# Pooled attention and a rational MoE layer: rest products in row halves, fill into open sums, moved due times

## The chip, the cores and the metric

The kernel runs on one core of a Trainium2 chip. The metric is the device time of one execution, in microseconds.

## The reference

Attention with pooled keys and values feeds one feed-forward layer with a rational function in the middle.

```python
B, H, S, D = 8, 8, 576, 64
k_p = k.reshape(B, H, 72, 8, D).mean(axis=3)           # eight neighbours become one key
v_p = v.reshape(B, H, 72, 8, D).mean(axis=3)
scores = (q @ k_p^T) / sqrt(D)
attn = exp(scores - max);  attn /= sum(attn) + 1e-9
x = (attn @ v_p) as [B*S = 4608 tokens, H*D = 512]
h = x @ w_in                                            # 512 -> 2048
P = a[0] + a[1]*h + a[2]*h^2 + a[3]*h^3
Q = 1 + |b[0]|*|h| + |b[1]|*h^2
out = (P / (Q + 1e-6)) @ w_out                          # 2048 -> 512
```

All arrays are float32 except the two weight matrices, which come as 64-bit floats.

## The kernel before

**Blocks and units.** The 4608 tokens are 18 blocks of 256. The 2048 hidden columns are 8 units of 256. The list `order` says which blocks meet which unit when: blocks 0 to 3 one by one at first, while the weights arrive, and from block 4 on (with block 1 again) in overlapping pairs, so that every block is in two neighbouring pairs, with four of the units in each. `mm1` multiplies a block (or a pair, 512 columns at once) with `w_in`, `rational` computes P/Q on ScalarE, VectorE and GpSimd, and `mm2` adds the products with `w_out` to the block's two open sums `po`, which `deliver` writes out at the end.

**Precision.** Products run in fp32r, a float32 format that TensorE takes in one pass. Where that is not precise enough a value is split into a high and a low part, and three products (high x high, low x high, high x low) are added. So `x`, the weights, `gh`/`gl`, the attention weights `am` and the pooled values `vm` all stand twice.

**Attention of a block.** `prep_k` and `prep_v` load and pool keys and values of a batch (`prep_v_early`, for the first two batches, lets TensorE do the pooling). `attention` computes scores `ps`, the softmax in tile `e`, and the transposed weights in `am` (by TensorE transposes for blocks 0 to 3, by VectorE's 32x32 transposes and DMAs after that). `values` multiplies them with the pooled values into the banks `pv`, and two copies by ScalarE and VectorE split the result into `x`.

**The rest of the keys.** Two heads share one product: 2 x 72 = 144 keys. 128 of them fill the array's rows, and the last REM = 16 are left over. For these rests there is a product of its own, whose 128 rows hold four copies (index g) of two pairs of heads (index m) of 16 rows (index r). The four copies hold the four combinations of high and low parts of weights and values, so that one product adds them all at once. Before, the rows are ordered (g, m, r). The product of one pair of heads uses all 128 rows with the other pair's masked to zero: `vr` has one masked version for each of the four pairs, made with the columns `mrem_lo` and `mrem` of `masks`. In `values`, for each half `c` of the heads, pair `jj` and batch segment, four products go to one `pv` bank: two with `vm`, one with `vr`, one with `vm`. A block that crosses a batch boundary has two segments, so its products are shorter and twice as many.

**What sets the order.** Nothing is issued in program order. `Plan.add` records each operation with its engine, an estimated cost, and a due time `plan.now`. `Plan.solve` first hands due times back to the operations that others depend on, then goes through time with those costs and picks for each engine the operation that can start first, with a small weight on due times. It also hands out the buffers: PSUM has 8 banks (pool `ps`), and an operation can start only when it gets all banks that it touches first. `Plan.issue` writes out the order, one in-order queue per engine; semaphores keep dependencies. Loads are all on SyncE's queue.

**Fill.** Where the plan has TensorE wait, `issue` puts in dummy products of 256 columns with the identity `identr` (`self.filler`), priced at 0.12 us. Up to the last operation on the bank `idle` (due at 96 us) they go into that bank, which nothing else can use until then; after that, up to FILL = 110 us of plan time, into a fresh bank just before the operation that will overwrite it.

Helper `Plan.issue` issues nearly everything, so most instructions carry line L267, and fill carries L264. They are told apart by tile.

Of the kernel before, what the change touches and what calls it, by code (L numbers as in the profile page):

```python
# [8 lines left out]
F32 = mybir.dt.float32  # L9
# [85 lines left out]
class Op:  # L95
    __slots__ = ("eng", "cost", "port", "calls", "deps", "users", "bufs", "due", "wait",
                 "ready", "seq", "bytes", "early", "slack", "start", "end")


class Plan:  # L100
# [5 lines left out]
    FILL = 110.0  # L106

    BETA = 0.02
# [13 lines left out]
    def add(self, eng, cost, calls, port=False, claims=(), bytes=0, early=34.0, after=()):  # L122
        op = Op()
        op.eng, op.cost, op.port, op.calls, op.bytes = eng, cost, port, calls, bytes
        op.early, op.slack = early, self.slack
# [24 lines left out]
        for b in op.bufs:  # L150
            b.left += 1
        self.ops.append(op)
        return op

    def solve(self):
        for op in reversed(self.ops):
            for d in op.deps:
                d.users.append(op)
                d.due = min(d.due, op.due - d.slack * (d.cost + 0.25 + (4.0 if d.bytes else 0.0)))
        for op in self.ops:  # L160
            op.wait, op.ready = len(op.deps), max(0.0, op.due - op.early)
# [9 lines left out]
        while done < len(self.ops):  # L171
# [58 lines left out]
            for u in op.users:  # L230
                u.wait -= 1
                u.ready = max(u.ready, op.end + (self.LAT if u.eng != op.eng else 0.0))
                if not u.wait:
                    engs[u.eng].append(u)
# [4 lines left out]
    def issue(self):  # L239
        for op in self.order:  # L240
            for b in op.bufs:
                b.it = None
        engines = {"sp": self.nc.sync, "act": self.nc.scalar, "actq": self.nc.scalar,
                   "dve": self.nc.vector, "pool": self.nc.gpsimd, "pe": self.nc.tensor}
        value = lambda v: v.ap() if isinstance(v, Lazy) else v
        free, steady = None, [o.start for o in self.order if self.idle.tile in o.bufs][-1]
        for op in self.order:
            if op.eng == "pe" and op.start <= self.FILL:


                to = self.idle.ap() if op.start <= steady else None
                dst = op.calls[0][1][0]
                if to is None and dst.tile.it is None and dst.tile.dtype == F32:
                    to = dst.ap()
                one = self.filler
                if to is not None and tuple(to.shape) != (128, 128):
                    one = one.unsqueeze(1).to_broadcast([128, 2, 128])
                    if tuple(to.shape) not in ((128, 256), (128, 2, 128)):
                        to = None
                while free is not None and to is not None:  # L260
                    free += 0.12 if free > self.WARM else 0.215
                    if free > op.start - (0.0 if op.start <= steady else 0.2):
                        break
                    self.nc.tensor.matmul(to, lhsT=self.filler, rhs=one, start=True, stop=True)  # L264
                free = op.end
            for name, args, kw in op.calls:
                getattr(engines[op.eng], name)(*map(value, args),  # L267
                                               **{k: value(v) for k, v in kw.items()})
# [17 lines left out]
def tile_pooled_attention_then_rational_moe(  # L286
# [21 lines left out]
    G = 8  # L308
# [57 lines left out]
    masks = new("cpool", "masks", [P, 6], F32, "masks")  # L366
# [6 lines left out]
    mrem_lo, mrem = ([masks[:, i + m:i + m + 1] for m in range(2)] for i in (2, 4))  # L373
# [6 lines left out]
    def make_masks():  # L380
# [12 lines left out]

        for m in range(2):
            for g in range(4):
                band(bands[:, g:g + 1], g * 32 + m * REM, g * 32 + (m + 1) * REM)
            small("tensor_tensor", out=mrem_lo[m], in0=bands[:, 1:2], in1=bands[:, 3:4],
                  op=ALU.add)
            small("tensor_tensor", out=mrem[m], in0=bands[:, 0:1], in1=bands[:, 2:3], op=ALU.add)
            small("tensor_tensor", out=mrem[m], in0=mrem[m], in1=mrem_lo[m], op=ALU.add)  # L400
# [65 lines left out]
    vr = [new("cpool", f"vr{i}", [P, NJ, D], F32R, f"vr{i}") for i in range(2)]  # L466

    def prep_k(n):
# [5 lines left out]
        for c0, c1, np in ((0, 2, P), (2, 4, P), (4, 5, H * SP - 4 * P)):  # L474
# [9 lines left out]
            while w > D:  # L484
# [34 lines left out]
    def prep_v_early(n):  # L519
# [11 lines left out]
        for m in range(2):  # L531
            dma(64, place[m * REM:(m + 1) * REM, CW:2 * CW].rearrange("p (c x) -> p c x", c=2),
                rows[m::2, 0:REM, :].rearrange("c r x -> r c x"))
# [5 lines left out]
    def prep_v(n):  # L539
# [4 lines left out]
        for c in (2, 0, 1):  # L544
# [4 lines left out]
            else:  # L549
                for g in range(4):  # L550
                    for m in range(2):
                        p0 = g * 32 + m * REM
                        dma(64, place[p0:p0 + REM].rearrange("p (j x) -> p j x", j=2),
                            rows[m::2, 0:REM, :].rearrange("c r x -> r c x"))
# [10 lines left out]
    def split_v(n, vs, vrs, port):  # L565
# [44 lines left out]
    def attention(t, hi, lo, qs, es):  # L610

# [50 lines left out]
        rem = [pairs[:, 2 * c:2 * c + 2, 0:REM].unsqueeze(1).to_broadcast([P, 4, 2, REM])  # L662
               for c in range(2)]
        four = [pairs[:, NJ + c, REM:].rearrange("p (g m r) -> p g m r", g=4, m=2)
# [6 lines left out]
        else:  # L671
# [6 lines left out]
            for c in range(2):  # L678
# [4 lines left out]
            act(2 * P).copy(lo[:, NJ:, col], pr)  # L683
            dve(2 * P).tensor_tensor(
                out=lo[P // 2:, NJ:, col], in0=pr[P // 2:],
                in1=lo[P // 2:, NJ:, col].bitcast(F32), op=ALU.subtract)
# [36 lines left out]
    def attend(i):  # L723
# [12 lines left out]
        if i >= 4:  # L736
# [171 lines left out]
    for g in range(4):  # L908
        small("tensor_copy", out=fourfold[:, g * 32:(g + 1) * 32], in_=ident[:2 * REM, :2 * REM])
# [29 lines left out]
    plan.filler = identr  # L939
# [38 lines left out]
```

## Time and profile before

| | |
|---|---|
| median of 3 runs | 952.7 us (952.23 to 953.07) |
| profiled execution | 953.93 us, its span 952.2 us |
| TensorE products busy | 938.5 us, 99% of the span |
| VectorE, ScalarE, GpSimd busy | 83%, 73%, 55% |
| products | 4888 records, 160 of them on tile `idle` |
| mean granted TensorE clock | 0.997 |

The span runs from the first to the last instruction of the profiled execution. In the views below PE is TensorE's products and PEld its weight loads, which overlap the products; DVE is VectorE, ACT ScalarE, POOL GpSimd and SP SyncE. Records of products overlap too: a product's record ends when its last result has left the array, well after the next has begun. What a product costs on a full TensorE is therefore the distance from its start to the next start, not its mean duration.

### The profile page before, as it was taken

Reading aid. Unit: us, or ns where it says so; the run is one execution under the profiler, and the core shown is the slowest. Engines: PE = TensorE matmul, PEld = TensorE weight load, DVE = VectorE, ACT = ScalarE, POOL = GpSimd, SP = SyncE. Lnnn points to the kernel's source line nnn. Section 1 sums busy time; section 2 is a strip of 40 time slices with the busy share of each in tenths; the row PEclk is TensorE's granted clock in tenths of the full one; section 3 lists DMA queues with packets and bytes.
Section 4 is the critical chain, followed back from the end, with each engine's and each line's share of the span. In section 5 each row is a group of like instructions: output and inputs, shape, how many; then the busy total and the mean of one; then the engine's idle time right before and its main releaser. Section 6 shows DMA issues by size and latency. Waiting matters only on the chain.

```text
span 952.2 us, 14488 instructions
## 1 busy us (share of the span) xinstructions
PE 938.5 (99%) x4888; PEld 786.1 (83%) x4888; DVE 791.5 (83%) x1334; ACT 691.6 (73%) x1124; POOL 523.3 (55%) x463
## 2 busy tenths in 40 slices
PE   8999999999999999999999999999999999999997
PEld 7989999898878888877887888878887888888886
DVE  6978888988898888888888989888979878886664
ACT  4778788687767686767777686858586868586764
POOL 4676667874456453547454844465456544444442
PEclk9999999999999999999999999999999999999999
DMA  9993110551436130316031512162223312020001
GB/s 280 345 384 120 24 50 1 120 149 49 89 64 148 19 60 12 66 51 141 5 68 50 122 33 43 41 135 55 32 53 74 71 26 53 0 56 1 23 1 45
DMA packets 185354, 75.16 MB, mean 79 GB/s; under 512 B 162624, under 2 KB 162624, under 8 KB 185280
## 3 DMA queue, kind: packets, MB, share of 16 engines
q1 hardware_dynamic: 185280, 74.23, 31.6%
q8 instruction: 39, 0.64, 0.3%
q14 instruction: 35, 0.29, 0.1%
HBM read 50.60 MB, written 12.58 MB: 66 GB/s over the span
## 4 chain that ended last, share of the span: by engine, by line
PE 84%; DVE 6%; ACT 3%; SPq 2%; DMA 2%; issue 2%; POOL 1%; ACTq 0%; POOLq 0%; DVEq 0%
PE po L267 37%; PE ph L267 36%; PE pv L267 4%; PE ps L267 3%; SPq L267 2%; DVE t L267 2%; PE idle L264 1%; DVE m_win L267 1%; DVE sm L267 1%; DMA q<-in_q_dram 1%; PE pvs L267 1%; DMA st_v<-in_v_dram 1%; DVE e L267 1%; ACT t L267 1%; ACT rp L267 1%
## 5 line engine op out<-in xcount | busy, mean ns | idle before, releaser
L267 PE MATMUL ph<-x,win 128*128 128x512 f32 (+1 forms) x2112 | 469.9, 354 | 4.8 <-DVE t L267 1.8
L267 PEld LDWEIGHTS ph<-x,win 128*128 128x128 f32 x2112 | 355.1, 188 | 72.6 <-DVE t L267 3.6
L267 PE MATMUL po<-wout,gh 128*128 128x512 f32 x1152 | 329.6, 397 | 0.3 <-ACT gh L267 0.3
L267 POOL TENSOR_TENSOR w<-w,r 128x512 f32<-128x512 f32 (+1 forms) x145 | 190.8, 1316 | 243.4 <-ACT r L267 228.9
L267 PEld LDWEIGHTS po<-wout,gh 128*128 128x128 f32 x1152 | 208.5, 188 | 42.1 <-ACT gh L267 0.5
L267 POOL TENSOR_TENSOR gl<-t,gh 128x512 fp32r<-128x512 f32 (+1 forms) x145 | 189.0, 1304 | 97.3 <-ACT gh L267 93.5
L267 PE MATMUL po<-wout,gl 128*128 128x512 f32 x576 | 167.6, 397 | 0.0
L267 ACT ACTIVATE t<-ph,abn 128x512 f32<-128x512 f32 (+1 forms) x145 | 111.7, 771 | 41.0 <-PE ph L267 30.8
L267 ACT ACTIVATE rp<-w,cbias 128x512 f32<-128x512 f32 (+1 forms) x145 | 99.7, 688 | 57.4 <-POOL w L267 24.3
L267 DVE TENSOR_TENSOR t<-t,ph 128x512 f32<-128x512 f32 (+1 forms) x145 | 98.4, 678 | 50.0 <-ACT t L267 48.0
L267 DVE SCALAR_TENSOR_TENSOR t<-t,abn,rp 128x512 f32<-128x512 f32 (+1 forms) x145 | 106.7, 736 | 35.2 <-ACT rp L267 33.8
L267 ACT ACTIVATE r<-w,abn 128x512 f32<-128x512 f32 (+1 forms) x145 | 117.7, 812 | 20.7 <-POOL gl L267 12.2
L267 PEld LDWEIGHTS po<-wout,gl 128*128 128x128 f32 x576 | 105.5, 189 | 21.9 <-issue 0.2
L267 DVE SCALAR_TENSOR_TENSOR t<-t,abn,ph 128x512 f32<-128x512 f32 (+1 forms) x145 | 107.5, 741 | 8.5 <-ACT w L267 4.7
L267 ACT ACTIVATE w<-ph 128x512 f32<-128x512 f32 (+1 forms) x145 | 85.9, 592 | 38.3 <-PE ph L267 29.8
L267 ACT CAST gh<-t 128x512 fp32r<-128x512 f32 (+1 forms) x145 | 88.4, 609 | 23.7 <-DVE t L267 23.4
L267 DVE SCALAR_TENSOR_TENSOR t<-rp,t 128x512 f32<-128x512 f32 (+1 forms) x145 | 99.0, 683 | 4.0
L267 DVE SCALAR_TENSOR_TENSOR rp<-w,rp 128x512 f32<-128x512 f32 (+1 forms) x145 | 99.2, 684 | 0.5 <-ACT rp L267 0.5
L267 ACT ACTIVATE rp<-rp 128x512 f32<-128x512 f32 (+1 forms) x145 | 84.1, 580 | 3.3 <-DVE t L267 0.5
L267 POOL TENSOR_TENSOR e<-e,sm 128x576 f32<-128x576 f32 x36 | 41.5, 1160 | 52.5 <-DVE sm L267 34.2
L267 PE MATMUL pv<-am,vm 128*128 128x256 f32 (+3 forms) x288 | 47.8, 278 | 0.5 <-ACT rp L267 0.4
L267 PEld LDWEIGHTS ps<-kpT,qT 128*128 128x128 f32 (+1 forms) x320 | 39.7, 178 | 9.5 <-issue 4.1
(95 smaller groups left out, 829.8 us busy)
## 6 DMA issues: line engine op xcount, KB each, us to landing
am<-e SPq DMA_DIRECT2D x224, 48.0 KB, 2.1
out_dram<-ob SPq DMA_DIRECT2D x17, 512.0 KB, 3.2
rwin<-in_moe_w_in_dram SPq DMA_DIRECT2D x8, 1024.0 KB, 11.8
rwout<-in_moe_w_out_dram SPq DMA_DIRECT2D x8, 1024.0 KB, 11.4
st_k<-in_k_dram SPq DMA_DIRECT2D x12, 512.0 KB, 4.8
st_v<-in_v_dram SPq DMA_DIRECT2D x12, 512.0 KB, 4.3
q<-in_q_dram SPq DMA_DIRECT2D x144, 32.0 KB, 2.1
st_v<-in_v_dram SPq DMA_DIRECT2D x48, 64.0 KB, 3.6
```

The source lines that it names most:

```text
L264: self.nc.tensor.matmul(to, lhsT=self.filler, rhs=one, start=True, stop=True)
L267: getattr(engines[op.eng], name)(*map(value, args), **{k: value(v) for k, v in kw.items()})
```

## The change

**Rest rows.** The 128 rows are reordered to (m, g, r): rows 0-63 hold the four copies of one pair of heads, rows 64-127 those of another. The pair jj of both halves c now share one chunk, one in the lower and one in the upper rows. The masked versions go: `vr` keeps two instead of four blocks of columns, and `split_v` makes it with one ScalarE and one VectorE operation instead of two of each. Loads, `fourfold`, `bands` and `masks` follow the new order. For the weights, one ScalarE and one VectorE operation over all 128 partitions, with a column `one_lo` of zeros and ones as scale, replace operations on half of the partitions.

**`values`.** Both `pv` banks of a block are now taken at once. The loops run over jj, segment, term and c. The rest products of c = 0 and c = 1 stand next to one another, each with 64 rows (K = 64) and its own bank.

**Fill.** Bank `idle` is given up at HEAD + 6 = 24 us of plan time. After that, fill multiplies zeros and adds them to the most recent open `po` sum, whenever one is open, through the whole kernel; the limit FILL goes.

**Due times.** `shift` adds up to ±4 us to the due time of 3% of the first 1850 operations, five times, with fixed seeds, after due times have been handed back.

**Lead.** From batch 3 on, the plan holds the transposes of pooled keys back by 1.5 us after their inputs.

```diff
 class Plan:
-    FILL = 110.0
     BETA = 0.02
+    MOVED, SHARE, REACH = 1850, 0.03, 4.0
+    SHIFTS = (570665, 613494, 158088, 911655, 140883)
...
+    def shift(self):
+        for seed in self.SHIFTS:
+            rnd = random.Random(seed)
+            for op in self.ops[:self.MOVED]:
+                if rnd.random() < self.SHARE:
+                    op.due += rnd.uniform(-self.REACH, self.REACH)
...
-                u.ready = max(u.ready, op.end + (self.LAT if u.eng != op.eng else 0.0))
+                u.ready = max(u.ready, op.end + u.lead + (self.LAT if u.eng != op.eng else 0.0))
...
     def issue(self):
-            if op.eng == "pe" and op.start <= self.FILL:
-                to = self.idle.ap() if op.start <= steady else None
-                dst = op.calls[0][1][0]
-                if to is None and dst.tile.it is None and dst.tile.dtype == F32:
-                    to = dst.ap()
-                one = self.filler
...
+            if op.eng == "pe":
+                if op.start <= steady:
+                    to, one, first = self.idle.ap(), self.filler, True
                     one = one.unsqueeze(1).to_broadcast([128, 2, 128])
+                elif sums:
+                    to, one, first = list(sums.values())[-1][:, 0:256].ap(), self.zeros, False
+                else:
+                    to = None
                 while free is not None and to is not None:
                     free += 0.12 if free > self.WARM else 0.215
-                    if free > op.start - (0.0 if op.start <= steady else 0.2):
+                    if free > op.start:
                         break
-                    self.nc.tensor.matmul(to, lhsT=self.filler, rhs=one, start=True, stop=True)
+                    self.nc.tensor.matmul(to, lhsT=self.filler, rhs=one, start=first, stop=first)
...
     prep_k:
-            pe(109 * nc_, [
+            turned = pe(109 * nc_, [
...
+            turned.lead = 1.5 if n > 2 else 0.0
...
     split_v:
-        r = vr[n % 2].rearrange("p (c m) x -> p c m x", m=2)
-        for m in range(2):
-            dst = r[:, :, m, :]
-            act(2 * D + 100).activation(dst, vrs, AF.Copy, scale=mrem_lo[m])
-            dve(2 * D, port=port).scalar_tensor_tensor(
-                out=dst, in0=vrs, scalar=mrem[m], in1=dst.bitcast(F32),
-                op0=ALU.mult, op1=ALU.subtract)
+        r = vr[n % 2]
+        act(2 * D + 100).activation(r, vrs, AF.Copy, scale=mrem_lo)
+        dve(2 * D, port=port).scalar_tensor_tensor(
+            out=r, in0=vrs, scalar=1.0 / G, in1=r.bitcast(F32), op0=ALU.mult, op1=ALU.subtract)
...
     attention:
-        rem = [pairs[:, 2 * c:2 * c + 2, 0:REM].unsqueeze(1).to_broadcast([P, 4, 2, REM])
+        rem = [pairs[:, c:NJ:2, 0:REM].unsqueeze(2).to_broadcast([P, 2, 4, REM])
...
     values:
-        for c in range(2):
-            pv = bank(f"pv{i}_{c}", [P, 2, TOK])
-            calls = []
-            for jj in range(2):
-                j = 2 * c + jj
-                for r0, r1, n in segs(i * TOK, TOK):
-                    vh, vl = vm[n % 2]
-                    o = pv[:, jj, r0:r1]
-                    terms = ((o, vh[:, j, :], hi[:, j, r0:r1]), (o, vl[:, j, :], hi[:, j, r0:r1]),
-                             (pv[:D, jj, r0:r1], vr[n % 2][:, j, :], lo[:, NJ + c, r0:r1]),
-                             (o, vh[:, j, :], lo[:, j, r0:r1]))
-                    calls += [mm(dst, vals, probs, s == 0, s == 3)
-                              for s, (dst, vals, probs) in enumerate(terms)]
-            pe(118 * len(calls), calls)
+        pvs = [bank(f"pv{i}_{c}", [P, 2, TOK]) for c in range(2)]
+        for jj in range(2):
+            calls = []
+            sg = segs(i * TOK, TOK)
+            for r0, r1, n in sg:
+                vh, vl = vm[n % 2]
+                for s, (vals, probs) in enumerate(((vh, hi), (vl, hi), (vr[n % 2], lo), (vh, lo))):
+                    for c in range(2):
+                        j = 2 * c + jj
+                        if s == 2:
+                            half = slice(c * (P // 2), (c + 1) * (P // 2))
+                            calls.append(mm(pvs[c][:D, jj, r0:r1], vals[half, jj, :],
+                                            probs[half, NJ + jj, r0:r1], False, False))
+                        else:
+                            calls.append(mm(pvs[c][:, jj, r0:r1], vals[:, j, :],
+                                            probs[:, j, r0:r1], s == 0, s == 3))
+            pe(118 * 7 * len(sg) + 10, calls)
...
     attend:
-            half = slice(P // 2, P)
-            act(2 * TOK).copy(lo[0:P // 2, NJ:], whole[0:P // 2, NJ:])
-            own = es[half, 0:2, :, 0:P]
-            both = [x[half, NJ:].rearrange("p c (m s) -> p c m s", m=2) for x in (lo, whole)]
-            act(2 * TOK).copy(own.bitcast(F32R), both[1])
+            own = es[:, 0:2, :, 0:P]
+            both = [x[:, NJ:].rearrange("p c (m s) -> p c m s", m=2) for x in (lo, whole)]
+            act(2 * TOK).activation(own.bitcast(F32R), both[1], AF.Copy, scale=one_lo)
...
-    plan.now = 96.0
+    plan.now = HEAD + 6.0
     plan.add("pe", 0, [mm(plan.idle[:, 0], ident, ident, True, True)], early=0.0)
...
+        nc.vector.memset(ones, 0.0)
+        nc.vector.tensor_copy(zero, ones[:, 0:1])
```

More of the change, by code (lines that the diff above doesn't have):

```diff
@@ L1 @@
+import random
 from contextlib import ExitStack
@@ L96 @@
     __slots__ = ("eng", "cost", "port", "calls", "deps", "users", "bufs", "due", "wait",
-                 "ready", "seq", "bytes", "early", "slack", "start", "end")
+                 "ready", "seq", "bytes", "early", "slack", "start", "end", "lead")
 class Plan:
@@ L124, in add @@
         op.eng, op.cost, op.port, op.calls, op.bytes = eng, cost, port, calls, bytes
-        op.early, op.slack = early, self.slack
+        op.early, op.slack, op.lead = early, self.slack, 0.0
         op.seq, op.due, op.deps, op.users = len(self.ops), self.now, set(), []
@@ L159, in solve @@
                 d.due = min(d.due, op.due - d.slack * (d.cost + 0.25 + (4.0 if d.bytes else 0.0)))
+        self.shift()
         for op in self.ops:
@@ L246, in issue @@
         free, steady = None, [o.start for o in self.order if self.idle.tile in o.bufs][-1]
+        sums = {}
         for op in self.order:
-            if op.eng == "pe" and op.start <= self.FILL:
-                to = self.idle.ap() if op.start <= steady else None
-                dst = op.calls[0][1][0]
-                if to is None and dst.tile.it is None and dst.tile.dtype == F32:
-                    to = dst.ap()
-                one = self.filler
-                if to is not None and tuple(to.shape) != (128, 128):
+            if op.eng == "pe":
+                if op.start <= steady:
+                    to, one, first = self.idle.ap(), self.filler, True
                     one = one.unsqueeze(1).to_broadcast([128, 2, 128])
-                    if tuple(to.shape) not in ((128, 256), (128, 2, 128)):
-                        to = None
+                elif sums:
+                    to, one, first = list(sums.values())[-1][:, 0:256].ap(), self.zeros, False
+                else:
+                    to = None
                 while free is not None and to is not None:
                     free += 0.12 if free > self.WARM else 0.215
-                    if free > op.start - (0.0 if op.start <= steady else 0.2):
+                    if free > op.start:
                         break
-                    self.nc.tensor.matmul(to, lhsT=self.filler, rhs=one, start=True, stop=True)
+                    self.nc.tensor.matmul(to, lhsT=self.filler, rhs=one, start=first, stop=first)
                 free = op.end
+                for name, args, kw in op.calls:
+                    if name == "matmul" and args[0].tile.name.startswith("po"):
+                        sums[id(args[0].tile)] = args[0]
+                        if kw["stop"]:
+                            del sums[id(args[0].tile)]
             for name, args, kw in op.calls:
@@ L365, in tile_pooled_attention_then_rational_moe @@
     ident = identr.bitcast(F32)
-    masks = new("cpool", "masks", [P, 6], F32, "masks")
+    zero = real([P, 1], F32R, tag="zero", name="zero")
+    masks = new("cpool", "masks", [P, 4], F32, "masks")
     fourfold = new("work1", "vs", [P, P], F32, "fourfold")[:2 * REM]
@@ L371, in tile_pooled_attention_then_rational_moe @@
     mlo, mhi = masks[:, 0:1], masks[:, 1:2]
-    mrem_lo, mrem = ([masks[:, i + m:i + m + 1] for m in range(2)] for i in (2, 4))
+    one_lo, mrem_lo = masks[:, 2:3], masks[:, 3:4]
     QC = 1.0 + 1e-6
@@ L392, in make_masks @@
         band(mhi, SP - REM, P)
-        for m in range(2):
[L395 to L400, printed above, removed]
+        for g in range(4):
+            band(bands[:, g:g + 1], (2 * g + 1) * REM, (2 * g + 2) * REM)
+        for g in (0, 2):
+            small("tensor_tensor", out=bands[:, g:g + 1], in0=bands[:, g:g + 1],
+                  in1=bands[:, g + 1:g + 2], op=ALU.add)
+        small("tensor_tensor", out=mrem_lo, in0=bands[:, 0:1], in1=bands[:, 2:3], op=ALU.add)
+        for m in range(2):
+            band(bands[:, m:m + 1], (4 * m + 2) * REM, (4 * m + 4) * REM)
+        small("tensor_tensor", out=one_lo, in0=bands[:, 0:1], in1=bands[:, 1:2], op=ALU.add)
+        small("tensor_scalar", out=one_lo, in0=one_lo, scalar1=float(G), scalar2=None,
+              op0=ALU.mult)
     WS = 2.0 ** 8
@@ L465, in tile_pooled_attention_then_rational_moe @@
           for i in range(2)]
-    vr = [new("cpool", f"vr{i}", [P, NJ, D], F32R, f"vr{i}") for i in range(2)]
+    vr = [new("cpool", f"vr{i}", [P, 2, D], F32R, f"vr{i}") for i in range(2)]
     def prep_k(n):
@@ L532, in prep_v_early @@
             dma(64, place[m * REM:(m + 1) * REM, CW:2 * CW].rearrange("p (c x) -> p c x", c=2),
-                rows[m::2, 0:REM, :].rearrange("c r x -> r c x"))
+                rows[2 * m:2 * m + 2, 0:REM, :].rearrange("c r x -> r c x"))
         st = place[:2 * REM, CW:2 * CW].rearrange("p (c t d) -> p t c d", c=2, t=G)
@@ L551, in prep_v @@
                     for m in range(2):
-                        p0 = g * 32 + m * REM
+                        p0 = (4 * m + g) * REM
                         dma(64, place[p0:p0 + REM].rearrange("p (j x) -> p j x", j=2),
-                            rows[m::2, 0:REM, :].rearrange("c r x -> r c x"))
+                            rows[2 * m:2 * m + 2, 0:REM, :].rearrange("c r x -> r c x"))
             w = RW // 2
@@ L661, in attention @@
         main = pairs[:, 0:NJ, REM:]
-        rem = [pairs[:, 2 * c:2 * c + 2, 0:REM].unsqueeze(1).to_broadcast([P, 4, 2, REM])
+        rem = [pairs[:, c:NJ:2, 0:REM].unsqueeze(2).to_broadcast([P, 2, 4, REM])
                for c in range(2)]
-        four = [pairs[:, NJ + c, REM:].rearrange("p (g m r) -> p g m r", g=4, m=2)
+        four = [pairs[:, NJ + c, REM:].rearrange("p (m g r) -> p m g r", g=4, m=2)
                 for c in range(2)]
@@ L904, in tile_pooled_attention_then_rational_moe @@
     pe(0, [mm(plan.idle[:, 0], ident, ident, True, True)])
-    plan.now = 96.0
+    plan.now = HEAD + 6.0
     plan.add("pe", 0, [mm(plan.idle[:, 0], ident, ident, True, True)], early=0.0)
     plan.now = 0.0
-    for g in range(4):
-        small("tensor_copy", out=fourfold[:, g * 32:(g + 1) * 32], in_=ident[:2 * REM, :2 * REM])
+    small("tensor_copy", out=fourfold.rearrange("p (m g r) -> p m g r", m=2, g=4),
+          in_=ident[:2 * REM, :2 * REM].rearrange("p (m r) -> p m r", m=2).unsqueeze(
+              2).to_broadcast([2 * REM, 2, 4, REM]))
     make_masks()
@@ L938, in tile_pooled_attention_then_rational_moe @@
         mm2(blocks, u, fs, gh, gl, halves)
-    plan.filler = identr
+    plan.filler, plan.zeros = identr, zero.to_broadcast([P, TOK])
     plan.solve()
```

6 lines of the change are left out of this document (3 added, 3 removed).

## The prediction

> **What bounds the kernel now.** I read the head of the page first, then the busy time by stretch, then the products by shape.
>
> ```profile
> span 952.2 us, 14488 instructions
> PE 938.5 (99%) x4888; PEld 786.1 (83%) x4888; DVE 791.5 (83%) x1334; ACT 691.6 (73%) x1124; POOL 523.3 (55%) x463
> ```
>
> TensorE is idle for 952.2 - 938.5 = 13.7 us, and no other engine is above 83%. The stretches say where the idle time is (columns: stretch, its length, busy us and records of PE, PEld, DVE, ACT, POOL, granted clock, DMA share, GB/s):
>
> ```profile
> 24.00:38.00 14.00, 12.70 (x106) 12.29 (x104) 13.04 (x22) 10.79 (x18) 9.64 (x7) 1.00 1.03 381
> 38.00:96.00 58.00, 57.50 (x417) 53.16 (x418) 49.31 (x78) 45.98 (x82) 40.41 (x31) 0.97 0.77 256
> 182.00:930.00 748.00, 744.11 (x3582) 609.78 (x3582) 629.37 (x1066) 544.98 (x880) 397.83 (x328) 1.00 0.27 58
> ```
>
> From 182 to 930 us TensorE lacks 3.9 us in 748, so there a product removed is time removed, and nothing on another engine is. Busy time in the head deceives, because fill counts in it. The same view of tile `idle` alone (PE, PEld, clock, DMA share, GB/s):
>
> ```profile
> 24.00:38.00 14.00, 2.12 (x14) 1.56 (x12) 1.00 1.03 381
> 38.00:96.00 58.00, 12.42 (x79) 10.80 (x79) 0.97 0.77 256
> 96.00:182.00 86.00, 0.38 (x2) 0.31 (x2) 1.00 0.19 48
> ```
>
> ```profile
> 39.21 2.99 PE L264 MATMUL idle<-identr 128*128 128x256 f32 x23
> 42.04 0.40 PE L267 MATMUL pv<-am,vm 128*128 128x256 f32 x2
> ```
>
> ```profile
> 51.27 0.63 PE L267 MATMUL po<-wout,gh 128*128 128x512 f32 x2
> ```
>
> The 23 fills take 42.04 - 39.21 = 2.83 us, 0.123 each. So 93 of them are 11.4 us, and with the idle 1.3 + 0.5 us the stretch 24 to 96 us holds 13.2 us in which TensorE does nothing useful. That is the second reserve; the first 24 us are start-up that the change hardly touches.
>
> **The rest products (`vr`), the part that repeats.** Before, each of 96 products runs alone. After, the same 96 stand as 48 pairs, one in rows 0-63 and one in rows 64-127, into different banks.
>
> ```profile
> L267 PE MATMUL pv<-am,vr 128*64 128x256 f32 x48 | 13.5, 281 | 0.0
> L267 PE MATMUL pv<-am,vr 128*64 128x192 f32 x16 | 4.0, 250 | 0.0
> L267 PE MATMUL pv<-am,vr 128*64 128x128 f32 x16 | 3.6, 224 | 0.0
> L267 PE MATMUL pv<-am,vr 128*64 128x64 f32 x16 | 3.6, 223 | 0.0
> ```
>
> Durations overlap, so the price is the distance to the next start. In the timeline (start, length, what):
>
> ```profile
> 414.38 0.28 PE L267 MATMUL pv<-am,vr 128*64 128x256 f32 x1
> 414.50 0.51 PE L267 MATMUL pv<-am,vm 128*128 128x256 f32 x3
> ```
>
> ```profile
> 315.11 0.25 PE L267 MATMUL pv<-am,vr 128*64 128x192 f32 x1
> 315.19 0.44 PE L267 MATMUL pv<-am,vm 128*128 128x192 f32 x3
> 315.47 0.22 PE L267 MATMUL pv<-am,vr 128*64 128x64 f32 x1
> 315.53 0.56 PE L267 MATMUL pv<-am,vm 128*128 128x64 f32 x3
> ```
>
> A `vr` product costs 0.12 us at 256 columns, 0.08 at 192 and 0.06 at 64; I take 0.06 at 128 too. If the two of a pair run side by side, one of each pair is saved: 24 x 0.12 + 8 x 0.08 + 8 x 0.06 + 8 x 0.06 = 4.5 us. No run here has two products in different rows. The nearest rows are scores of a tile that crosses a batch, where two products use different columns:
>
> ```profile
> 276.86 0.85 PE L267 MATMUL ph<-x,win 128*128 128x512 f32 x3
> 277.64 0.71 PE L267 MATMUL ps<-kpT,qT 128*64 128x144 f32 x8
> 278.28 0.73 PE L267 MATMUL ph<-x,win 128*128 128x512 f32 x2
> ```
>
> ```profile
> 371.70 0.65 PE L267 MATMUL ps<-kpT,qT 128*128 128x144 f32 x4
> 372.10 1.19 PE L267 MATMUL ph<-x,win 128*128 128x512 f32 x4
> ```
>
> Eight half records take 0.64 us where four whole ones take 0.40; singly, at the whole ones' 0.10, they would take 0.80 and more. So halves do overlap, but something is paid: the three `ph` at 0.23 would end at 277.55, and the halves start at 277.64. The same at the one kind of product with half the rows, a transpose of keys:
>
> ```profile
> 52.54 0.74 PE L267 MATMUL ph<-x,win 128*128 128x256 f32 x5
> 53.22 0.27 PE L267 MATMUL pl<-identr,ks 64*128 64x64 f32 x1
> 53.42 0.50 PE L267 MATMUL ph<-x,win 128*128 128x256 f32 x2
> ```
>
> and, for the weight loads of `ps` and `vr`:
>
> ```profile
> 277.64 0.44 PEld L267 LDWEIGHTS ps<-kpT,qT 128*64 128x64 f32 x8 [0.36 <-issue]
> 414.27 0.13 PEld L267 LDWEIGHTS pv<-am,vr 128*64 128x64 f32 x1
> ```
>
> Five `ph` at 0.118 end at 53.13; `pl` starts 0.09 later. The second `ph` after it starts at 53.42 + 0.50 - 0.28 = 53.64, 0.51 after 53.13; less its neighbour's 0.12 and a slot of about 0.11 for `pl` itself, the visit costs 0.28 us extra. The PEld rows show why: the weights of `ps` come after 0.36 us without a load, while those of `vr` (414.27) go in behind the product before, which starts at 414.38 - 0.12 = 414.26. So the two ends for a pair at 256 columns are -0.12 us (no visit cost) and -0.12 + 0.28 = +0.16.
>
> Which end? `pl` and `ps` are plain float32, `vr` is fp32r. With half the columns `ps` pays and `vr` does not, in the same shape 128*64. The products that are moved are `vr`, so I take the row of their own type: no visit cost, -4.5 us. What the row cannot tell is whether `vr`, which begins at column 0 and is alone, counts as half an array at all; that keeps the other end alive as the first rival.
>
> The Trainium skill, "TensorEngine Tiling (Array Packing)", Key Properties, says that changing the tiling mode, not just the tile, drains the engine. By that rule the sum would be the first rival's; the trace agrees at `pl` and `ps` and not at `vr`.
>
> **The head: bank of `idle`, due times, fill.** The fill bank is held until about 24 us instead of 96, so eight banks serve the stages in between; 1850 of the planner's operations get five draws of up to 4 us on 3% each. The ends: all 13.2 us saved, or a loss, since an order moved at random can also put a wait first. The bank alone can save little where the end is set by a chain, as before 42.04, where the last transposes had to be split first. If that chain (2.83 us) and the idle 1.8 us stay, 8.6 us are left to save; some of it will, and I take a third, -3.0 us; bounds -8.6 and +2.8.
>
> The draws move loads on SP's queue too. With the DMA engines full from 24 to 38 us (share 1.03, 381 GB/s), a 1 MB weight load that goes ahead puts another 1 / 0.381 = 2.8 us back; that is the loss at the upper end.
>
> After 24 us there is no fill until an output sum is open, first at 51.27 us above. TensorE then stands idle at 39 to 42 us, unless work moves there. The clock can drop for it:
>
> ```profile
> 59.60:63.10 3.50, 3.50 (x12) 3.05 (x13) 2.07 (x5) 2.61 (x5) 3.50 (x2) 0.51 1.05 406
> ```
>
> A drop of this kind runs 3.5 us at 0.51, so it costs at most 3.5 x 0.49 = 1.7 us. One is there already and may go or stay, so I take 0, with ends of ±1.7.
>
> **Fill after 96 us.** Now fill goes wherever the plan has a gap. Only 2 fills are in 96 to 182 us and none later, where TensorE lacks 3.9 us: a fill in a real gap is free, one too many costs 0.12. At one for every gap of 0.3 us, 13 x 0.12 = 1.6 us is the end; I take +0.3.
>
> **`values` order, copies, masks, lead.** Both sums of a block finish together, so the first copy can no longer run beside the second half.
>
> ```profile
> L267 ACT CAST x<-pv 128x512 fp32r<-128x512 f32 x36 | 21.0, 582 | 5.6 <-PE pv L267 5.0 <-PE ph L267 0.4
> ```
>
> The waits (us, times, longest), and a change of blocks in the timeline:
>
> ```profile
> PE ph L267 <- ACT x L267: 1.1, 1, 1.1
> PE pk L267 <- DVE ks L267: 0.2, 1, 0.2
> ```
>
> ```profile
> 369.38 1.10 PE L267 MATMUL po<-wout,gh 128*128 128x512 f32 x4
> 370.32 1.09 PE L267 MATMUL po<-wout,gl 128*128 128x512 f32 x4
> 371.24 0.62 PE L267 MATMUL ph<-x,win 128*128 128x512 f32 x2
> ```
>
> The extra copy, 0.58 us, is hidden by eight `po` (1.9 us between 369.38 and 371.24). If banks are short, `pv` waits for two at once; `po` beside it is the cover. Only the first block has none: there `ph` waited 1.1 us for `x` and will wait 0.6 more, of which I count +0.5. One ACT copy of half the partitions goes in each of the 14 late blocks, four small ACT and DVE operations per pair of batches, and some GpSimd set-up; the DMAs keep number and size. None is on TensorE's path: 0. The two new set-up writes on VectorE come before the first keys land: 0. The lead of 1.5 us moves the transposes of later keys behind other products; they waited 0.2 us on record, so -0.2, with ends of -1 and +0.5.
>
> **Sum.** -4.5 - 3.0 + 0 + 0.3 + 0.5 - 0.2 = -6.9 us. The profiled execution took 953.93 us, 1.7 around its span and 1.2 over the median; taken from the median of 952.7 this is 945.8, rounded to 946.
>
> **Rivals.** First, the other sign: each pair pays the visit. Place: all 48 pairs, each between whole-array products. Price: 0.28 for each, 13.4 us, less the 4.5 saved: +8.9 instead of -4.5. With the other terms (-2.4) it gives 959. It decides from a visit of (4.5 + 2.4) / 48 = 0.14 us on; `pl` and `ps` speak for it, `vr` against.
>
> Second: halves run one after the other without a visit cost, and the pair is worth nothing: 952.7 - 2.4 = 950. For it: no trace row has two row halves. Against: the column halves overlap.
>
> The Trainium skill, "TensorE: Matmul & The Clock Gate", Part 3, says that products in different row groups start within about 4 ns of one another. By that rule the second rival falls; no run here shows it.
>
> Third: pairs gain 4.5, but the head loses (a clock drop of 1.7, moved loads +2.8): 952.7 - 4.5 + 0.6 + 4.5 = 953.3, no change.
>
> **Chances.** Forecast 0.48 (941 to 949), first rival 0.30 (954 to 961), second 0.14 (946 to 953), third 0.08. The range 941 to 959 leaves out the upper half of the first rival and a little below, some 0.2. What a measurement of this kernel can tell from no change is about 0.2%, 1.9 us. Faster: 0.47 from the forecast, 0.12 from the second rival, 0.04 from the first, where the head saves nearly all of its 13.2 us. Same: 0.01 + 0.02 + 0.05 from forecast, second and third. Slower: 0.26 + 0.03 from first and third.
>
> **What would show it.** If right, the timeline has two `vr` records of 64*64 within 0.01 us, the next product 0.12 us after, and weights loaded without a gap. If the first rival holds, PEld stands idle some 0.3 us before each pair, and the product after it comes 0.3 us late. In the head, the count of `idle` records after 24 us goes to nearly none, and fill on `po` with TensorE's idle time there sums to about 10 us instead of 13.2. The clock column shows whether 38 to 42 us stays at 1.00. I am wrong altogether if TensorE is idle for more than 4 us between 182 and 930 us, by waits for two banks.

## The result, and the profile after

| | before | after |
|---|---|---|
| median | 952.9 us (4 runs) | 967.2 us (964.4 to 969.0, 4 runs) |
| ratio, 95% interval | | 1.0145 [1.0117, 1.0173] |
| profiled execution, its span | 953.93, 952.2 us | 967.07, 965.3 us |
| mean granted TensorE clock | 0.997 | 0.995 |

The change costs 14.3 us where 6.7 were forecast as gain. The head of the page after:

```profile
span 965.3 us, 14351 instructions
PE 948.1 (98%) x4845; PEld 785.4 (81%) x4845; DVE 792.9 (82%) x1328; ACT 682.2 (71%) x1102; POOL 522.8 (54%) x453
```

TensorE is as full as before with 43 records fewer, all of them fill (160 before, 75 on `idle` and 42 on `po` after), so the time is in what the records cost. By stretch (us, busy time and records of PE, PEld, DVE, ACT, POOL, granted clock, DMA share, GB/s):

```profile
24.00:38.00 14.00, 8.25 (x57) 7.00 (x56) 12.19 (x22) 8.60 (x15) 9.56 (x6) 0.95 1.04 387
38.00:96.00 58.00, 57.27 (x403) 51.55 (x402) 51.73 (x80) 48.70 (x81) 41.57 (x31) 0.98 0.76 253
182.00:930.00 748.00, 744.72 (x3522) 604.94 (x3521) 619.60 (x1050) 526.37 (x845) 390.87 (x324) 1.00 0.26 58
```

TensorE lacks 3.3 us between 182 and 930, where before lacked 3.9. But fill into open sums now stands in that stretch and counts as busy: 28 records, 28 x 0.12 = 3.4 us. With it, 6.7 us there are without use, 2.8 more than before. The rest products by shape, and one full block in the timeline, products and then weight loads (start, length, what):

```profile
L283 PE MATMUL pv<-am,vr 64*64 64x256 f32 x48 | 8.2, 326 | 0.6 <-DVE am L283 0.6
L283 PE MATMUL pv<-am,vr 64*64 64x192 f32 x16 | 2.5, 309 | 0.0
```

```profile
420.76 0.63 PE L283 MATMUL pv<-am,vm 128*128 128x256 f32 x4
421.32 0.33 PE L283 MATMUL pv<-am,vr 64*64 64x256 f32 x2
421.58 0.98 PE L283 MATMUL pv<-am,vm 128*128 128x256 f32 x6
422.49 0.33 PE L283 MATMUL pv<-am,vr 64*64 64x256 f32 x2
422.74 0.51 PE L283 MATMUL pv<-am,vm 128*128 128x256 f32 x2
423.09 1.09 PE L283 MATMUL po<-wout,gl 128*128 128x512 f32 x4
```

```profile
420.53 0.66 PEld L283 LDWEIGHTS pv<-am,vm 128*128 128x128 f32 x4
421.32 0.13 PEld L283 LDWEIGHTS pv<-am,vr 64*64 64x64 f32 x2
421.58 0.77 PEld L283 LDWEIGHTS pv<-am,vm 128*128 128x128 f32 x6
```

The two halves do run at once: the group of two is 0.33 us long, no more than one of its records, and in 45 of the 48 pairs the second starts 3 or 4 ns after the first (12 to 223 ns in the other three). But the visit has a price on both sides. Four `vm` at 0.118 would end at 421.23, and the pair starts at 421.32. The next `vm` starts 0.26 after the pair, and the six of them take 0.91 until the next pair where 6 x 0.118 is 0.71. From pair to pair that is 1.17, so a pair costs 1.17 - 0.71 = 0.46 us where two whole products cost 0.24. The weight loads show it too: PEld stands still from 421.19 to 421.32 and from 421.45 to 421.58, so the loads that otherwise hide behind products lie open. The excess is 0.22 for each of the 48 pairs: 10.6 us.

**Where the 13.1 us between the two spans come from.** Pairs +10.6. Two stretches at half clock in the middle, shown below, about +3.4. Between 182 and 930 us: the 28 fills, of 42 in all, where before had none, +3.4; TensorE's idle time -0.6. The head from 24 to 96 us: 6.5 idle and 23 fills make 9.3 us without use where before had 13.2, -3.9. The sum is +12.9.

### The profile page after: what moved, and what is told of

Its sections match the earlier page's. It is cut to its first block, busy times and chain, and to the rows that moved or that the text cites. A ratio compares the mean times of both kernels' runs of the same rounds, so it can differ in the third digit from the quotient of the medians.

```text
span 965.3 us, 14351 instructions
## 1 busy us (share of the span) xinstructions
PE 948.1 (98%) x4845; PEld 785.4 (81%) x4845; DVE 792.9 (82%) x1328; ACT 682.2 (71%) x1102; POOL 522.8 (54%) x453
## 4 chain that ended last, share of the span: by engine, by line
PE 86%; DVE 7%; SPq 2%; ACT 2%; issue 1%; DMA 1%; POOL 1%; DVEq 0%; ACTq 0%; POOLq 0%
PE po L283 37%; PE ph L283 37%; PE pv L283 5%; PE ps L283 4%; SPq L283 2%; DVE t L283 2%; DVE sm L283 1%; DMA q<-in_q_dram 1%; PE pvs L283 1%; DVE e L283 1%; DVE m_win L283 1%; DVE m_wout L283 0%; DVE rp L283 0%; ACT rp L283 0%; PE pm L283 0%
## 5 line engine op out<-in xcount | busy, mean ns | idle before, releaser
L283 POOL TENSOR_TENSOR gl<-t,gh 128x512 fp32r<-128x512 f32 (+1 forms) x145 | 192.2, 1326 | 101.3 <-ACT gh L283 90.6
L283 PEld LDWEIGHTS po<-wout,gh 128*128 128x128 f32 x1152 | 210.7, 189 | 43.6 <-issue 0.2
L283 PE MATMUL po<-wout,gl 128*128 128x512 f32 x576 | 169.7, 399 | 0.0
L283 PE MATMUL ps<-kpT,qT 128*128 128x144 f32 (+1 forms) x320 | 47.1, 293 | 2.7 <-DVE kpT L283 1.3
```

What stands on the lines that cost most here:

```text
L283: getattr(engines[op.eng], name)(*map(value, args), **{k: value(v) for k, v in kw.items()})
```

## The experiments

"Before" was run beside each (medians 952.5 to 953.1); ratios are to it. The theory after the result was that each visit of half rows among whole products costs TensorE a drain (the products before it have to finish first) and open weight loads. The rivals: the order that the plan makes of it, both banks taken at once, the draws, the late fill.

**The plan of after, whole rows (`e1_whole_rows`).**

```diff
-    calls.append(mm(pvs[c][:D, jj, r0:r1], vals[half, jj, :], probs[half, NJ + jj, r0:r1], ...
+    calls.append(mm(pvs[c][:D, jj, r0:r1], vals[:, jj, :], probs[:, NJ + jj, r0:r1], ...
```

> The changed kernel with the same plan and the same order; only the rest products read all 128 rows again, as two products one after the other instead of a pair of halves. (The masks are not put back, so each rest product also adds the other pair's rest.) Theory 1, the visits: each pair of halves drains the array before and after, 0.22 us net of what it saves, 48 pairs, 10.6 us, and two drops of the clock behind them, 3.4 us. Then this kernel takes 967.2 - 14 = 953, between 951 and 956, the weights of the rests load without a gap, and the clock drops in the middle are gone. Theory 2, the order: waits for two banks at once, fill and moved due times cost the 14 us; then it stays at 963 or more.

Measured: 956.7 us, 1.0042 [1.0027, 1.0057]: 10.5 us below after, though the two products of a pair now take a slot each; 0.7 above the expected range. Its timeline, and its middle:

```profile
416.52 0.63 PE L283 MATMUL pv<-am,vm 128*128 128x256 f32 x4
416.99 0.40 PE L283 MATMUL pv<-am,vr 128*64 128x256 f32 x2
417.22 0.87 PE L283 MATMUL pv<-am,vm 128*128 128x256 f32 x6
417.94 0.40 PE L283 MATMUL pv<-am,vr 128*64 128x256 f32 x2
```

```profile
182.00:930.00 748.00, 741.93 (x3574) 609.81 (x3575) 626.04 (x1058) 531.32 (x853) 393.94 (x326) 1.00 0.26 58
```

From `vr` to `vr` now pass 0.95 us for eight products, 0.119 each, against 1.17 for seven slots. So most of the loss is in the visit itself, not in the order around it. The 3.8 us that remain over before belong to other parts of the change: in the middle TensorE lacks 6.1 us here beside 28 fills of 3.4, 9.5 us where before lacked 3.9, and the head gives part of that back.

**A whole product between the halves (`e2_halves_apart`).**

```diff
...
+    op.calls = [calls[k + x] for k in range(0, len(calls), n) for x in (0, 1, 2, 3, 4, 6, 5, 7)]
```

> The changed kernel with the same plan, but in each pair a whole product (high x low, c = 0) stands between the two halves: 96 visits of the array's halves instead of 48, and no half beside another. Theory 1: a visit costs 0.33 us beside the slot, so 48 more visits are 48 x 0.33 = 16 us, and 48 slots that no longer overlap 4 us: 985 to 990. Theory 2: only the overlap is lost, 4.5 us: 972.

Measured: 995.4 us, 1.0443 [1.0409, 1.0477], 28 us over after for 48 visits more, 0.59 each, and above the expected range.

```profile
433.47 0.63 PE L283 MATMUL pv<-am,vm 128*128 128x256 f32 x4
434.03 0.33 PE L283 MATMUL pv<-am,vr 64*64 64x256 f32 x1
434.29 0.38 PE L283 MATMUL pv<-am,vm 128*128 128x256 f32 x1
434.61 0.33 PE L283 MATMUL pv<-am,vr 64*64 64x256 f32 x1
434.86 0.85 PE L283 MATMUL pv<-am,vm 128*128 128x256 f32 x5
```

Each half is now a visit: 0.58 from one half to the next over one whole product (0.12), so 0.46 again, for a single half. 48 x 0.46 = 22 us. The mean clock fell too, from 0.995 to 0.982, worth at most 13 us; how the 28 split between the two stays open.

**One half alone (`e7_half_alone`).** The rest of c = 1 is left out.

```diff
+                            if c:
+                                continue
```

> The changed kernel with the same plan, the rest products of c = 1 (rows 64-127) left out, so a half in rows 0-63 stands alone in each visit. Theory 1: a half alone drains as a pair does, and the second half rides free: a full block's products for the values take 2.3 us as with the pairs, 965 to 969. If the halves of a pair ran one after the other, or a half from row 0 on did not drain: 2.1 us or less, 956 to 962.

```profile
419.90 0.63 PE L283 MATMUL pv<-am,vm 128*128 128x256 f32 x4
420.46 0.33 PE L283 MATMUL pv<-am,vr 64*64 64x256 f32 x1
420.72 0.98 PE L283 MATMUL pv<-am,vm 128*128 128x256 f32 x6
421.62 0.33 PE L283 MATMUL pv<-am,vr 64*64 64x256 f32 x1
421.88 0.51 PE L283 MATMUL pv<-am,vm 128*128 128x256 f32 x2
422.22 1.10 PE L283 MATMUL po<-wout,gl 128*128 128x512 f32 x4
```

Measured: 965.4 us in one run, within the spread of after. The block takes 422.22 - 419.90 = 2.32 us with one half and 2.33 with two: the second half is free, the visit is what costs.

**The type (`e8_rest_as_float32`).** Before's whole rest products, in float32.

```diff
-   (pv[:D, jj, r0:r1], vr[n % 2][:, j, :], lo[:, NJ + c, r0:r1]),
+   (pv[:D, jj, r0:r1], vr[n % 2][:, j, :].bitcast(F32), lo[:, NJ + c, r0:r1].bitcast(F32)),
```

> The kernel before with the rest products taken as plain float32 instead of fp32r, in the same shape (128 rows, 64 columns from column 0). float32 takes two passes, 0.12 us more for each of 96, 12 us: 965 if a part of the columns costs nothing whatever the type. If the type decides, as I took it from the scores, each of the 96 also pays a visit of 0.3 us, 29 us: 994, with a gap in the weight loads before each.

Measured: 1002.6 us, one run, about 50 over before. Products, then weight loads:

```profile
434.56 0.40 PE L267 MATMUL pv<-am,vm 128*128 128x256 f32 x2
434.89 0.65 PE L267 MATMUL pv<-am,vr 128*64 128x256 f32 x2
435.46 0.63 PE L267 MATMUL pv<-am,vm 128*128 128x256 f32 x3
```

```profile
434.89 0.19 PEld L267 LDWEIGHTS pv<-am,vr 128*64 128x64 f32 x2
435.46 0.42 PEld L267 LDWEIGHTS pv<-am,vm 128*128 128x128 f32 x3 [0.39 <-issue]
```

A float32 product is two records. They take 0.57 us, 0.24 of it for two slots and 0.33 beyond them, in the very shape 128*64 that costs nothing beyond its slot in fp32r. So with half the columns it is the type that decides.

**After without halves (`e4_no_halves`).** Before's masks, `vr` and `values`; after's fill, bank `idle` to 24 us, draws and lead.

> The kernel before with all of the change except the row halves: bank of fill given up at 24 us, fill into open sums, draws, lead; rest products, their masks and the order of the products for the values as before. Theory 1: the row halves are the whole loss, the others gain a little, 948 to 952. Theory 2: fill and due times carry the loss, 957 or more.

Measured: 950.9 us (10 runs), 0.9978 [0.9969, 0.9988]: this beats both kernels, by 2.0 us and 16.3 us. Bank, fill, draws and lead together are worth 2 us. The 16.3 belong to all that was left out: the halves, their masks and both banks at once.

**Halves alone (`e6_halves_only`).** After with before's plan, fill and due times, no draws and no lead.

> The kernel before with the row halves alone: new order of the rest rows, both sums of a block at once, pairs of halves; fill, due times and lead as before. Theory 1, the visits: 952.9 + 10.6 for the visits + 2 to 5 for drops of the clock behind them + 0 to 4 for two banks at once = 966 to 972. Theory 2, the loss lies in the new fill and due times: 958 or less.

Measured: 982.6 us, 1.0308 [1.029, 1.0325], 29.7 us over before, far more than the pairs' 10.6.

```profile
182.00:930.00 748.00, 734.20 (x3446) 595.16 (x3445) 617.33 (x1042) 519.11 (x831) 386.58 (x319) 0.99 0.27 58
```

```profile
PE pv L268 <- DVE t L268: 5.2, 2, 4.3
```

TensorE lacks 13.8 us in the middle instead of 3.9. `pv` waits 5.2 us in two places (sum, times, longest) where before had 0.4. The longer of the two, in the timeline:

```profile
749.26 0.28 PE L268 MATMUL pv<-am,vm 128*128 128x256 f32 x1
753.83 0.62 PE L268 MATMUL pv<-am,vm 128*128 128x256 f32 x3 [4.29 <-DVE t L268]
```

The first product of the block goes into its bank, and the second, which goes to the other bank, waits 4.29 us for a VectorE operation that reads a `ph` bank and whose result `pv` does not use: a wait for the second bank. The visits' 10.6, the 9.9 us more without work and the clock come to about the 29.7: the trace has four stretches of the middle at half clock, 17 us together, worth at most 8.5.

**Both sums at once, whole rows (`e9_both_sums`).** `e4_no_halves` with both `pv` banks taken at once and the products alternating between them; all eight of a segment are priced.

> The kernel of e4 (all of the change but the row halves), with one thing of `values` put in: both sums of a block are taken at once and their products alternate, with whole rest products at their true price. If taking two banks at once is a cost of its own, as the idle 18 us of e6 after 182 us and the 3.8 us that e1 stays above the kernel before suggest, this takes 5 to 15 us more than e4: 956 to 966. If those waits came from the halves and the wrong price of the pairs, it stays at 951 to 953.

Measured: 967.7 us, 1.0156 [1.0141, 1.0171], 16.8 over `e4_no_halves` without one half row, and above the expected range. The fill marks where the plan has TensorE wait (tile `zero`: record lengths, first and last start; `e9_both_sums`, then `e4_no_halves`):

```profile
L275 PE MATMUL po<-zero,identr x121: 271/274/367, 75.5 to 644.3; 128*128 128x256 f32 x121
```

```profile
L275 PE MATMUL po<-zero,identr x45: 270/274/377, 78.3 to 194.4; 128*128 128x256 f32 x45
```

In its timeline, one of the gaps:

```profile
282.50 0.64 PE L283 MATMUL po<-wout,gl 128*128 128x512 f32 x2
282.98 2.73 PE L275 MATMUL po<-zero,identr 128*128 128x256 f32 x23
285.55 0.28 PE L283 MATMUL pv<-am,vm 128*128 128x256 f32 x1
```

76 more fills are 9.1 us, and from 24 to 930 us TensorE is idle for 13.3 us instead of 8.8: waits are 13.6 of the 16.3 us between the two spans. 23 of the fills, 2.6 us, stand right before a `pv`. After, with the same two banks, has only 42 fills, and 58 without its draws (`e3_no_draws`). So the two banks can make waits, and the order decides how many. How much of the 16.8 is the banks, and how much comes from draws that were picked for another order, stays open.

**The draws.** `SHIFTS = ()` in after (`e3_no_draws`) and in `e4_no_halves` (`e10_no_halves_no_draws`); in `e11_more_draws` `e4_no_halves` gets 14 seeds more, picked for an end 2.1 us earlier by the plan's own costs.

> The changed kernel without the five random draws on due times. If the draws bring the head what they bring the plan, this takes 2 to 4 us longer: 969 to 971. If the chip does not follow, 966 to 968. Theory 1 and theory 2 differ little here: by theory 2, with the moved due times as cause, it would be faster by 5 us or more.

> The kernel of e4 without the draws on due times: what bank, fill and lead bring alone. The draws shorten its plan by 1.8 us. If the chip follows, 952.5; if not, 950.5 to 951.5, as e4.

> The kernel of e4 with fourteen more draws, kept because each shortens the plan, 2.1 us together; row halves stay out. If the chip follows the plan as it did from the kernel before to e4 (2.9 us in the plan, 2.0 on the chip), 949 to 950; if such small steps are lost on the chip, 951.

Measured: 969.3 us, 1.0156 [1.0128, 1.0183]; 956.1, 1.0034 [1.0021, 1.0047]; 961.3, 1.0085 [1.0061, 1.0109]. In after no effect of the draws is shown (the intervals overlap). In `e4_no_halves` they are worth 5.2 us, but 14 more, better by plan, cost 10.4, some 5 of it by the clock, which is at half for 10.2 us of the head in that profile. What random draws give by the plan does not carry over to the chip in size, nor always in sign.

**Fill from 24 us to the first open sum (`e12_gap_fill`).** `e10_no_halves_no_draws` has no fill there; this adds fill into the bank that the next operation will overwrite.

```diff
-                    to = None
+                    to, one, first = None, self.filler, True
+                    dst = op.calls[0][1][0]
+                    if dst.tile.it is None and dst.tile.dtype == F32:
+                        to = dst.ap()
...
```

> The kernel of e10 with the same plan and order, and fill put back into the stretch from 24 us to the first open sum (into the bank that the next operation is about to overwrite, as the kernel before did). In e10 the clock is at half from 40.8 to 47.7 us. If the missing fill is the cause, that stretch stays at full clock and 3.4 us come back: 952 to 953.5. If the drop comes from the order, or fill there holds up real products, 955 to 957.

Measured: 953.9 us (10 runs), 1.0014 [1.0003, 1.0024], 2.2 below `e10_no_halves_no_draws` with the same order. The same stretch of the two (clock third from last), without the fill and with it:

```profile
40.80:47.70 6.90, 6.10 (x23) 5.46 (x24) 6.24 (x10) 4.60 (x9) 3.62 (x6) 0.51 1.13 279
```

```profile
40.80:47.70 6.90, 6.90 (x54) 6.64 (x53) 6.83 (x11) 5.08 (x9) 3.83 (x6) 1.00 1.14 270
```

Without fill the clock is halved for 6.9 us. The gap in the fill is a real, if small, price of giving up bank `idle`. How much of the 2.2 us is the clock stays open: one of the five runs without that fill had a mean clock of 1.000 and still took 955.5 us.

**No late fill (`e5_no_late_fill`).** After without zeros into open sums.

```diff
-                elif sums:
+                elif sums and False:
```

> The changed kernel with the same plan, without the fill into open sums (fill into the bank of its own until 24 us stays). 42 records of that fill take 6.2 us, 3.6 of them after 150 us. If they stand where TensorE would wait anyway, nothing changes: 966 to 968. If they delay real products after 150 us, 963.5. If the clock needs them at 77 to 90 us, one more drop there, 968.5.

Measured: 967.2 us, 1.0155 [1.0138, 1.0172], the same as after. The 28 fills of the middle stand in gaps that are there without them, and this run shows the gaps bare:

```profile
182.00:930.00 748.00, 741.58 (x3488) 600.51 (x3488) 620.04 (x1049) 525.90 (x843) 390.38 (x323) 1.00 0.26 57
```

TensorE lacks 6.4 us here, 1.9 of it in one wait of the second `pv` product of a block, as in `e6_halves_only`.

## Why the prediction was wrong

**The step that failed** is "Which end? ... The products that are moved are `vr`, so I take the row of their own type: no visit cost". It put the visit at nothing, and a visit costs 0.46 us where two whole products cost 0.24. Half of the reasoning was true: fp32r with half the columns pays no visit, float32 does (`e8_rest_as_float32`). But the change halves rows, and there fp32r pays as `pl` did (`e1_whole_rows`, `e2_halves_apart`, `e7_half_alone`). The nearest row was the one of the same halved dimension, not that of the same type. The Trainium skill, "TensorEngine Tiling (Array Packing)", Key Properties, says that changing the tiling mode drains the engine; the trace agrees for half rows, with 0.46 us a visit, and shows no drain for fp32r with half the columns; whether that shape counts as another mode at all, no run here tells.

**Sizes.** The forecast had -4.5 us for the pairs; they cost +10.6, which is 15.1 of the 21.2 us between forecast and median. The other 6.1 lie in the other terms, forecast at -2.4 together and measured at 14.3 - 10.6 = +3.7: clock and waits in the middle took more than the head gave. The first rival had mechanism and place right and gave 959: it took 0.28 for the visit and gets 0.46 - 0.12 = 0.34, 2.9 us more over 48; with that and the two clock drops below it would have given 965. Its sign that PEld stands still 0.3 us before a pair came as 0.13 before and 0.13 after. The second rival falls: halves in different rows start together, 3 or 4 ns apart.

**The clock.** Taken as 0 with ends of ±1.7. Between the two profiled executions one drop in the head (59.6 before) was replaced by another (36.7, so 38 to 42 us did not stay at 1.00), and net the term was right. But the drop before was chance: 38 of the 41 runs of before that stand beside the experiments have a mean clock of 0.999 or 1.000, which leaves no room for it, since 1.7 of 952 us are 0.002. The drops in the middle were not thought of:

```profile
36.70:40.10 3.40, 3.40 (x17) 3.40 (x17) 1.03 (x2) 1.30 (x5) 3.40 (x4) 0.50 1.04 399
...
224.40:227.80 3.40, 3.40 (x10) 2.63 (x10) 1.60 (x4) 2.68 (x5) 2.02 (x2) 0.50 0.00 0
572.60:576.00 3.40, 3.40 (x11) 2.65 (x12) 0.61 (x2) 2.27 (x4) 0.78 (x1) 0.50 0.00 0
```

Half of 3.4 us is 1.7 for each. In the timeline, ahead of the first of the two:

```profile
222.79 0.27 PE L283 MATMUL pv<-am,vr 64*64 64x128 f32 x2
223.00 0.88 PE L283 MATMUL pv<-am,vm 128*128 128x128 f32 x6
223.81 0.27 PE L283 MATMUL pv<-am,vr 64*64 64x128 f32 x2
224.01 0.44 PE L283 MATMUL pv<-am,vm 128*128 128x128 f32 x2
224.29 1.04 PE L283 MATMUL po<-wout,gl 128*128 128x512 f32 x2
```

TensorE is never idle there. Both drops come right behind a block that crosses a batch, with four visits in some 4 us. `e1_whole_rows` has no drop in its middle. The runs of after also rank by clock: 0.998 took 964.4 us, 0.993 took 969.0. That visits cause the drops is not shown. For it: drops in the middle stand only in profiles with half rows (after and `e2`, `e3`, `e5`, `e6`), most of them right behind such a block. Against: `e7_half_alone` has 48 visits and none, in one run, and in `e3`, `e5` and `e6` some come behind waits of 1.7 to 4.3 us instead. `e8_rest_as_float32`, with the visits of float32, ran at 1.00.

**The head.** -3.0 forecast; the unused time went from 13.2 to 9.3 us, -3.9, with "about 10" named as the sign. 9 records on `idle` are left, as foretold. Of what is left, one wait on GpSimd is the largest (us, times, longest), not seen before, where it was 0.2:

```profile
PE pm L283 <- POOL e L283: 3.9, 1, 3.9
```

It has no fill in it, ends at 36.5 us, and the drop at 36.7 stands right behind it. The prediction's price for a moved load, 1 / 0.381, is 2.6 us as it is written; the load's 1024 KB give the 2.8.

Not all of the gain reaches the end: with the halves out, the whole of bank, draws, fill and lead is 2.0 us (`e4_no_halves`), and without the draws the rest is a loss of 3.2 (`e10_no_halves_no_draws`).

**`values` order.** +0.5, with "`po` beside it is the cover": wrong as a rule. In after it came out small, 2.8 us more without use in the middle. The sign for it, more than 4 us idle by waits for two banks, did not show in after's 3.3 because the fill covered it; bare it is 6.4, 1.9 of it shown to be such a wait (`e5_no_late_fill`). In `e6_halves_only` and `e9_both_sums`, both with this step, the waits grow by 9.9 and 13.6 us; at least the 4.3 at `pv` in `e6` are a wait for the second bank.

**Late fill** (+0.3): right in that no difference shows (`e5_no_late_fill`), though 28 fills came where 13 were reckoned as the end, since the gaps grew. Copies, masks and lead (0 and -0.2) weren't separated.

## What to carry to other kernels

Before packing products into parts of the array, find what one visit costs among whole products: two halves at once gain nothing here, since the visit costs more than the slot that they save. Either many such products share one visit (all rests of a block in one visit wasn't tried), or they stay whole. Take the price of an unseen shape from the row that shares its halved dimension, and treat its type as a second question. Where an order is found by a search on estimated costs, undo each part by itself on the chip: here the plan's 2.1 us for the better was 10.4 for the worse, and the best version measured was the change without its main part.

## What the hardware showed that was not expected

- Half rows cost a visit in fp32r (0.46 us for one half or two), half columns none (0.12 a product); in float32 half columns cost 0.33 beyond their slots (one run).
- The clock was halved for 3.4 us with no idle time of TensorE in the trace, right behind four visits of half rows, in two places of after. The Trainium skill, "TensorE: Matmul & The Clock Gate", Part 1, ties the halved clock to an idle window of about 3.4 us; the length agrees, the idle window was not there.
